# One core, fused Sinkhorn attention and ResMLP: reordering batch 0's loads, mixing and scoring, with other TensorE fillers

## The chip, the cores and the metric

The kernel runs on one core of one Trainium2 chip. The metric is the device time of one launch in microseconds (us). One core has five engines that run beside each other: TensorE (PE in the profile, with its weight loads shown apart as PEld), VectorE (DVE), ScalarE (ACT), GpSimd (POOL) and SyncE (SP). SP and POOL also issue the transfers (DMAs) from and to the chip's memory.

## What is computed

Four batches, eight heads, 768 positions, head size 64. For each head an 8x8 matrix goes through five rounds of a Sinkhorn normalisation; the result P mixes the eight blocks of 96 keys and of 96 values, each block of queries then attends to its own mixed block, and the output goes through a ResMLP block that mixes tokens and then channels.

```python
for _ in range(5):
    P = exp(P - max(P)); P = P / sum(P, -1); P = P / sum(P, -2)
k_sorted = einsum('bhij,bhjcd->bhicd', P, k_b)      # v_sorted the same
attn = softmax(scale * q_b @ k_sb.T)                 # inside each block of 96
x = (attn @ v_sb)  as (batch, 768, 512)
a1 = alpha1 * x + beta1
u = x + lam * einsum('ts,bsd->btd', w_tok, a1)
out = u + lam * (relu((alpha2 * u + beta2) @ w_ch1) @ w_ch2)
```

## The kernel before

The whole program is unrolled by Python: one straight list of instructions for each engine, which runs in the order in which the code issues it (the `Engine` wrapper at the top keeps that order). An engine waits at an instruction until its operands and its target buffer are free, and everything behind it on that engine waits too. There is no planner for batch 0: the order of its work is written out by hand at the end of the setup, from `mix_keys(0, psb)` down to `scale_affine(betaB)`. From there on a table (`put`, `run`) hangs the work of the next batch on the matmul groups of the present one: `h_unit` (the first channel product, 16 groups for each half of a batch) and `ch_unit` or `ch_pair` (the second).

Matmul results land in PSUM. Two pools hand out its tiles: psA has two slots of two banks, psB four slots of one bank. A new tile waits until the tile that last had its slot has been read.

Batch 0 goes through these steps, whose names the prediction uses:

- **Loads.** POOL issues the DMAs of q, k, v (each in two parts), of the token weights `wt16` (four parts), of alphaB, betaB and lamB, of W1p and W2p (four parts each) and of batch 1. All go into one queue. At most eight are under way, since a DMA that takes up the counter of an earlier one waits until that has landed.
- **Sinkhorn.** Five rounds, each one exponential on ACT and six small DVE operations. The table `beside` puts other work behind each round: `q_first` (24 small matmuls turn one group of queries), `q_out` (ACT copies them out), `mask` (DVE builds small masks from the identity), `prep_ab2`, and fillers.
- **Mixing.** `mix_keys` and `mix_values` make the matrices bigK and bigV from P. `k_turn` (24 matmuls of 64x64 for each of four groups) turns and mixes keys, `k_copy` copies them out. `v_sort` reorders the loaded values into VD in slices of eight or more of the 64 columns, `v_mix` (16 matmuls for each of eight slices) mixes them and copies them out to Vs.
- **Scores.** `score(0, g, half)` is eight matmuls and one exponential on ACT. There are four groups (pairs of heads) with two halves each. `pv_first(g)` is 24 matmuls that weight the values of a group, then a reciprocal and a multiplication on DVE that give x.
- **Token mixing.** `permute` reorders `wt16` into wp, `wtok` turns it (three matmuls) and copies it to w_tokT; `row_sum` and `row_sums` make the sums of the rows of the token weights; `first_mm`, `first_turn` and `first_finish` make, for one quarter of the channels at a time, the token product (tok_ps), the scaled input z and their sum a2T, which the first `h_unit` needs. `first_mm(3)` and `first_turn(3)` come after the first three h matmuls.
- **Fillers.** `warm(n)` and `fill` are matmuls of a tile of zeros, 128x512 in fp16, whose result nobody reads. They keep TensorE busy.

Before the change POOL issues k ahead of v, then makes the mask ebh, and does two of the four `v_sort` slices between the weight loads. ACT does two slices, and sums the rows of half of the token weights with three accumulating copies. DVE does the last slice and all the permuting. The eight `v_mix` stand between the scores of groups 0 to 2.

Of the kernel before, what the change touches and what calls it, by code (L numbers as in the profile page):

```python
# [16 lines left out]
def kernel(  # L17
# [111 lines left out]
    ebh = const([BH, B, 2, H, NB], F16, "ebh")  # L129

    def heads():
        for th in range(2):
            pool.tensor_copy(
                ebh[:, :, th, :, :],
                ident16[0:BH, 0:BH].rearrange("p (b h) -> p b h", h=H).unsqueeze(3).to_broadcast([BH, B, H, NB]),
            )
# [9 lines left out]
    )  # L146
    dve.memset(brow[:].bitcast(FT), 0.0)
    dve.memset(rrow[:].bitcast(FT), 0.0)
    load_slabs(k8, k)
    load_halves(v8, v[0])  # L150
    heads()
# [25 lines left out]
    pool.dma_start(alphaB[:], moe_alpha1.partition_broadcast(128))  # L177
    pool.dma_start(betaB[:], moe_beta1.partition_broadcast(128))
    pool.dma_start(lamB[:], moe_lam.partition_broadcast(128))
    v_sort(16, 32, pool.tensor_copy)  # L180
    for g in range(4):
        if g == 1:
            v_sort(48, 64, pool.tensor_copy)
        pool.dma_start(W1p[:, :, g * 512:(g + 1) * 512], w1v[:, :, g * 512:(g + 1) * 512])
    pool.tensor_tensor(brow[0:1, :], bet1[:], lam1[:], ALU.mult)

# [24 lines left out]
    def mask(n):  # L211
        if n == 0:
            dve.tensor_copy(ident16f[:], ident16[0:4 * CT, 0:4 * CT])
            dve.tensor_reduce(mlo[:], ident16[:].rearrange("p (b j) -> p j b", j=NB), AXX, ALU.add)
        elif n == 1:
            dve.tensor_reduce(msk[:], ident16[:].rearrange("p (b j) -> p b j", j=NB), AXX, ALU.add)
            dve.tensor_tensor(mhi[:], msk[:, 0:8], msk[:, 8:16], ALU.add)
            dve.tensor_reduce(mth[:], ident16[:].rearrange("p (th c) -> p th c", th=2), AXX, ALU.add)
        elif n == 2:
            dve.tensor_reduce(  # L220
                mgap[:], ident16[:].rearrange("p (th t) -> p th t", th=2)[:, :, 0:HB],
                mybir.AxisListType.XY, ALU.add,
            )

    def fill(out, n):
        for _ in range(n):
            pe.matmul(out, wz[:, 0:128], wz[:], start=True, stop=True)

# [45 lines left out]
    rcol = const([128, 3], FT, "rcol")  # L274

    def row_sum(m):
        if m == 0:
            a1_of[0] = moep.tile([128, 8, C], F16, name="a1", tag="a1", bufs=1)
        act.activation(a1_of[0][:].rearrange("p k c -> p (k c)")[:, 0:S], wt16[0][:, m, :], AF.Copy, accum_out=rcol[:, m:m + 1])


# [8 lines left out]
    def q_out(g):  # L290
        for half in range(2):
            q_copy(0, g, qps[g], half, act.copy)

    beside = {
        0: [lambda: q_first(0), lambda: warm(3)],
        1: [lambda: q_first(1), lambda: warm(2), lambda: warm(3)],
        2: [lambda: q_first(2), lambda: warm(3)],
        3: [lambda: q_out(0), lambda: q_first(3)],
        4: [lambda: q_out(1), lambda: q_out(2), lambda: q_out(3), lambda: prep_ab2(psb), lambda: warm(4)],
    }  # L300
    warm(12)
    for it in range(5):
        act.activation(P32[:], P32[:], AF.Exp)
        dve.tensor_reduce(rsum[:], P32[:], AXX, ALU.add)
        dve.reciprocal(rsum[:], rsum[:])
        dve.tensor_tensor(
            P32[:], P32[:], rsum[:].unsqueeze(2).to_broadcast([BH, NB, NB]), ALU.mult
        )
        dve.tensor_reduce(csum[:], P32[:].rearrange("p i j -> p j i"), AXX, ALU.add)
        dve.reciprocal(csum[:], csum[:])  # L310
        dve.tensor_tensor(
            (P16 if it == 4 else P32)[:], P32[:],
            csum[:].unsqueeze(1).to_broadcast([BH, NB, NB]), ALU.mult,
        )
        if it < 3:
            with nc.allow_low_precision(reason="sums of zeros and a one"):
                mask(it)
        for f in beside[it]:
            f()

    for g in range(4):
        pool.dma_start(W2p[:, g * 4:(g + 1) * 4, :], w2v[:, g * 4:(g + 1) * 4, :])

# [3 lines left out]
    def mix_keys(b, ps):  # L327
        rep = ps([128, H4, NB * NB], FT, "repk_ps")
        big = att.tile([128, H4, 64], F16, name="bigK", tag="bigK", bufs=2)
        for g0 in range(0, H4, 2):  # L330
            gs = slice(g0, g0 + 2)
            for g in range(g0, g0 + 2):
                for h2 in range(2):
                    n = b * H + 2 * g + h2
                    pe.matmul(
                        rep[h2 * 64:h2 * 64 + 64, g, :], ident16[0:BH, n:n + 1].to_broadcast([BH, 64]),
                        P16[:].rearrange("p i j -> p (i j)"), start=True, stop=True,
                    )
            sel = att.tile([128, 2 * NB, NB], FT, name="selk", tag="selk", bufs=2)
            dve.tensor_tensor(  # L340
                sel[:], rep[:, gs, :].rearrange("p g (i j) -> p (g i) j", j=NB),
                mhi[:].unsqueeze(1).to_broadcast([128, 2 * NB, NB]), ALU.mult,
            )
            red = att.tile([128, 2 * NB], FT, name="redk", tag="redk", bufs=2)
            dve.tensor_reduce(red[:], sel[:], AXX, ALU.add)
            dve.tensor_tensor(
                big[:, gs, :].rearrange("p g (i c) -> p (g i) c", c=NB),
                red[:].unsqueeze(2).to_broadcast([128, 2 * NB, NB]),
                mlo[:].unsqueeze(1).to_broadcast([128, 2 * NB, NB]), ALU.mult,
            )  # L350
        bigK[b] = big

    def mix_values(b, ps):
        rep = ps([128, NB * NB], FT, "repv_ps")
        pe.matmul(
            rep[:], ebh[:, b, :, :, :].rearrange("p a h j -> p (a h j)"),
# [4 lines left out]
            sel[:], rep[:].rearrange("p (i j) -> p i j", j=NB),  # L361
            mlo[:].unsqueeze(1).to_broadcast([128, NB, NB]), ALU.mult,
        )
        red = att.tile([128, NB], FT, name="red", tag="red", bufs=2)
        dve.tensor_reduce(red[:], sel[:], AXX, ALU.add)
# [3 lines left out]
            red[:].unsqueeze(1).to_broadcast([128, H, NB]), ALU.mult,  # L369
# [33 lines left out]
    def v_mix(b, n, ps, eng):  # L403
        ps = ps([128, 8, 64], FT, "v_ps")
        fill(ps[:].rearrange("p d x -> p (d x)"), 1 - n % 2)
        for s in range(8):
            for th in range(2):
# [3 lines left out]
                    ps[r, d, :], VD[r, n * 8 + d, :],  # L411
                    bigV[b][r, :, :].rearrange("p h i -> p (h i)"), start=True, stop=True,
                )
        eng(Vs[:, :, n * 8:(n + 1) * 8], ps[:].rearrange("p d x -> p x d"))
# [4 lines left out]
    def score(b, g, hf, ps):  # L419
        ps = ps([128, 2, 512], FT, "sc_ps")  # L420
        n = 128 if b == 0 else BLK
        keys = kT_of[b][:].rearrange("p g i t -> p (g i t)")
        for ii in range(4):
# [3 lines left out]
            for h2 in range(2):  # L427
                r = slice(h2 * 64, h2 * 64 + 64)
                pe.matmul(
                    ps[0:w, h2, ii * BLK:(ii + 1) * BLK], keys[r, lo:lo + w],  # L430
# [4 lines left out]
        act.activation(  # L435
            et[0:n].rearrange("p a i t -> p a (i t)"), ps[0:n, :, 0:4 * BLK], AF.Exp, scale=scale
        )
# [175 lines left out]
    def row_sums(ps):  # L613
        rc16 = const([128, 3], F16, "rc16")
        act.copy(rc16[:], rcol[:])
        ps = ps([1, 384], F16, "rr_ps")
        for m in range(3):
            pe.transpose(ps[:, m * 128:(m + 1) * 128], rc16[:, m:m + 1], ident16[:])
# [273 lines left out]

    mix_keys(0, psb)
    warm(3)
    mix_values(0, psb)
    prep_scales()
    dve.tensor_copy(Vs[:, :, D:GRP], mgap[:].unsqueeze(2).to_broadcast([128, H * NB, GRP - D]))
    kp0 = k_turn(0, 0, psb)
    kp1 = k_turn(0, 1, psb)
    k_copy(0, 0, kp0, 0, copy)  # L900
    k_copy(0, 0, kp0, 1, act.copy)
    warm(3)
    kp2 = k_turn(0, 2, psb)
    k_copy(0, 1, kp1, 0, copy)
    k_copy(0, 1, kp1, 1, act.copy)
    kp3 = k_turn(0, 3, psb)
    k_copy(0, 2, kp2, 0, copy)
    k_copy(0, 2, kp2, 1, act.copy)
    v_sort(0, 8, act.copy)
    v_sort(8, 16, act.copy)  # L910
    score(0, 0, 0, psa)
    k_copy(0, 3, kp3, 0, copy)
    k_copy(0, 3, kp3, 1, copy)
    score(0, 0, 1, psa)
    v_sort(32, 48, copy)
    warm(2, psb)
    v_mix(0, 0, psb, copy)
    v_mix(0, 1, psb, copy)
    score(0, 1, 0, psa)
    v_mix(0, 2, psb, copy)  # L920
    v_mix(0, 3, psb, act.copy)
    score(0, 1, 1, psa)
    v_mix(0, 4, psb, copy)
    v_mix(0, 5, psb, copy)
    score(0, 2, 0, psa)
    v_mix(0, 6, psb, copy)
    v_mix(0, 7, psb, act.copy)
    score(0, 2, 1, psa)
    row_sum(0)
    permute(0, copy, 0, 3)  # L930
    moe_start(0)
    warm(1, psb)
    pv_first(0)
    score(0, 3, 0, psa)
    wtok(0, copy)
    wtok(1, act.copy)
    wtok(2, copy)
    permute(0, copy, 3, 6)
    row_sum(1)
    row_sum(2)  # L940
    pv_first(1)
    wtok(3, copy)
    wtok(4, copy)
    wtok(5, copy)
    permute(1, copy, 0, 6)
    score(0, 3, 1, psa)
    pv_first(2)
    row_sums(psb)
    first_mm(0, psb)
    first_turn(0, psb)  # L950
    first_mm(1, psb)
    pv_first(3)
    first_turn(1, psb)
# [32 lines left out]
    for b in range(1, B):  # L986
        p = b - 1
        if b == 1:
            for n in range(3):
                put(0, 0, "h", 11 + n, lambda n=n: mix_v(1, n, act.copy))  # L990
                put(0, 0, "c", 3 + 3 * n, lambda n=n: mix_k(1, n, (act.copy,) * 4))
            put(0, 0, "h", 13, lambda: bounce_v(1))
# [112 lines left out]
```

## Time and profile before

| what | value |
|---|---|
| time, median of 3 runs | 258.61 us (258.02 to 258.95) |
| time of the profiled execution | 258.66 us |
| its span, first to last instruction | 256.9 us |
| outside the span | 1.8 us |
| PE busy | 246.9 us, 96% |
| DVE busy | 175.9 us, 68% |
| ACT busy | 155.3 us, 60% |
| POOL busy | 47.5 us, 18% |
| granted TensorE clock, mean | 0.997 |
| data moved by DMA | 31.07 MB, 121 GB/s over the span |

All times in the text are us from the start of the span, unless they are called durations. A line of the timeline gives the start, the duration, the engine, the operation with its tiles (result on the left of the arrow), the shape, the count of instructions merged into the line, and in brackets how long the engine stood idle before it and what it waited for. "issue" means that nothing the profile shows held the engine.

### The profile page before, as it was taken

To read this page: it belongs to the slowest core of one execution; us is meant where nothing else is said; L and a number is where in the kernel's file an instruction comes from. 1 tells how busy PE (TensorE), PEld (TensorE's weight loads), DVE (VectorE), ACT (ScalarE), POOL (GpSimd) and SP (SyncE) were. 2 spreads that over 40 slices of the span, in tenths; PEclk is the share of its full clock that TensorE was granted. 3 is DMA by queue.
4 is the path that set the end of the run, shared out by engine and by line. 5 is a ranking of instruction groups with operands and counts; after the bars stand their busy time and mean duration, and the time that the engine had idled before them with its cause. 6 is when DMAs were issued, how large, how long until landed. Compare 5 with 4: busy or idle time off the path is not lost.

```text
span 256.9 us, 5960 instructions
## 1 busy us (share of the span) xinstructions
PE 246.9 (96%) x2371; PEld 160.0 (62%) x2371; DVE 175.9 (68%) x467; ACT 155.3 (60%) x282; POOL 47.5 (18%) x73
## 2 busy tenths in 40 slices
PE   8998799999999999999999999999999999999994
PEld 2565565555555545456865787557756875686783
DVE  6696888594538956759896775298886873361873
ACT  3557767484997688496655587877465004847400
POOL 8859302810092010091000010000000000000000
PEclk9999999999999999999999999999999999999998
DMA  5999999997989997999972259910202232111023
GB/s 99 211 204 194 207 207 212 212 146 170 178 175 183 122 192 139 177 165 148 159 133 62 41 151 136 149 40 3 84 0 41 64 97 70 23 39 43 3 82 82
DMA packets 67535, 31.07 MB, mean 121 GB/s; under 512 B 56674, under 2 KB 63218, under 8 KB 67508
## 3 DMA queue, kind: packets, MB, share of 16 engines
q0 software_dynamic: 26832, 17.70, 46.9%
q1 hardware_dynamic: 40580, 12.97, 30.9%
q8 instruction: 18, 0.29, 0.5%
q14 instruction: 9, 0.07, 0.1%
q10 hardware_dynamic: 96, 0.03, 0.1%
HBM read 32.79 MB, written 8.65 MB: 161 GB/s over the span
## 4 chain that ended last, share of the span: by engine, by line
PE 81%; DVE 11%; ACT 4%; issue 2%; DVEq 0%
PE h_ps L65 28%; PE tok_ps L65 11%; PE px L65 8%; PE ch_ps L65 7%; PE pz L65 6%; PE py L65 5%; PE warm_ps L65 4%; PE x_ps L65 3%; DVE x L65 3%; PE sc_ps L65 2%; DVE ost L65 2%; DVE sums L65 2%; PE mix_ps L65 2%; PE kmix_ps L65 1%; PE v_ps L65 1%
## 5 line engine op out<-in xcount | busy, mean ns | idle before, releaser
L65 PE MATMUL h_ps<-a2T,W1p 128*128 128x384 bf16 x512 | 93.3, 326 | 0.0
L65 PEld LDWEIGHTS <-W1p 128*128 128x128 bf16 x512 | 47.9, 98 | 31.4 <-issue 0.4
L65 ACT ACTIVATE hTa<-h_ps 128x384 f16<-128x384 f32 x64 | 31.2, 493 | 30.3 <-PE h_ps L65 29.2
L65 ACT ACTIVATE hTb<-h_ps 128x384 f16<-128x384 f32 x64 | 31.2, 490 | 7.5 <-PE h_ps L65 7.5
L65 DVE SCALAR_TENSOR_TENSOR u<-tok_ps,x 128x512 f32<-128x512 f32 x21 | 14.5, 691 | 25.6 <-PE tok_ps L65 25.6
L65 PE MATMUL tok_ps<-a,w_tokT 128*128 128x512 f16 x126 | 30.3, 379 | 0.0
L65 ACT CAST kT<-kmix_ps 64x512 f16<-64x512 f32 x36 | 25.7, 713 | 5.7 <-PE kmix_ps L65 5.4
L65 ACT ACTIVATE et<-sc_ps 96x768 f16<-96x768 f32 (+1 forms) x32 | 24.8, 807 | 3.7 <-PE sc_ps L65 3.7
L65 ACT CAST u<-u 128x512 f16<-128x512 f32 x21 | 13.0, 618 | 21.3 <-DVE u L65 21.3
L65 PEld LDWEIGHTS <-sums 128*128 128x128 f16 x216 | 21.1, 98 | 3.5 <-issue 0.5
L65 PEld LDWEIGHTS <-hTa 128*128 128x128 f16 x192 | 18.4, 98 | 6.7
L65 PEld LDWEIGHTS <-hTb 128*128 128x128 f16 x200 | 18.6, 98 | 6.1
L65 PEld LDWEIGHTS <-w_tokT 128*128 128x128 f16 x126 | 12.3, 98 | 13.1 <-issue 0.2
L65 DVE TENSOR_TENSOR x<-x_ps,rcb 96x512 f16<-96x512 f32 x24 | 16.5, 686 | 0.8
L65 POOL DMA_DIRECT2D qn<-in_q_dram x18 | 16.0, 909 | 4.4 <-DMA raw<-in_v_dram 4.3
L65 DVE TENSOR_TENSOR sums<-hTa,hTb 128x512 f16<-128x512 f16 (+2 forms) x27 | 8.9, 330 | 10.3 <-ACT hTb L65 10.0
L65 PEld LDWEIGHTS <-et 96*128 96x128 f16 (+4 forms) x288 | 12.0, 100 | 4.7 <-DVE x L65 1.2
L65 PE MATMUL x_ps<-Vs,et 96*128 96x65 f16 (+4 forms) x288 | 13.0, 195 | 1.6 <-DVE x L65 0.9
L65 DVE SCALAR_TENSOR_TENSOR ost<-px,u 128x256 f32<-128x256 f32 x27 | 11.3, 419 | 3.4 <-PE px L65 3.4
L65 PE MATMUL warm_ps<-wz 128*128 128x512 f16 x36 | 11.8, 464 | 1.2 <-DVE wz L65 1.2
L65 POOL DMA_DIRECT2D vscr<-mixed x6 | 3.3, 557 | 48.0 <-ACT mixed L65 48.0
L65 PE MATMUL ch_ps<-W2p,hTb 128*128 128x512 f16 x48 | 11.8, 379 | 0.0
(140 smaller groups left out, 361.4 us busy)
## 6 DMA issues: line engine op xcount, KB each, us to landing
out_dram<-ost SPq DMA_DIRECT2D x23, 192.0 KB, 2.2
raw<-in_v_dram POOLq DMA_DIRECT2D x6, 384.0 KB, 7.4
raw<-in_k_dram POOLq DMA_DIRECT2D x6, 384.0 KB, 9.2
qn<-in_q_dram POOLq DMA_DIRECT2D x18, 128.0 KB, 10.6
vscr<-mixed POOLq DMA_DIRECT2D x6, 384.0 KB, 5.1
Vs<-vscr SPq DMA_DIRECT2D x3, 768.0 KB
W1p<-in_moe_w_ch_dram POOLq DMA_DIRECT2D x4, 512.0 KB, 11.2
W2p<-in_moe_w_ch_dram POOLq DMA_DIRECT2D x4, 512.0 KB, 17.1
```

The source lines that it names most:

```text
L65: ins = getattr(self.eng, name)(*args, **kwargs)
```

## The change

Only batch 0 and the setup are touched, and one detail of the mixing that all batches share.

- **Loads.** v is issued ahead of k. ACT makes the masks, a new one for the keys (ebk) among them, in place of POOL, between the first and the second exponential of the Sinkhorn rounds. alphaB, betaB, lamB, W1p and W2p are issued later on POOL, behind three `v_sort` slices and the product brow.
- **Fillers.** `slow(n)` is new: n matmuls of the same zeros read as fp32, 128x512. `slow(2)` and one `warm` take the place of the first twelve `warm`; single `slow(1)` stand beside rounds 1 to 3; `slow(2)` stands behind the scores of group 0. Of the other fillers one `warm` is left.
- **Mixing.** `mix_values` comes first. `mix_keys` works on all four groups at once (four matmuls and three DVE operations on 256 columns, where there were eight and six on 128). Their sums are kept in PSUM.
- **Values.** ACT sorts four slices of eight columns, POOL one of sixteen and two of eight. The matmuls of all eight slices (`v_mm`) and their copies (`v_out`, two slices in one copy once) come ahead of the scores, between the turns of the keys.
- **Scores.** Group 0 is scored between and behind the turns of the last keys, the other groups later. Four of the eight halves use two psB slots and two exponentials of 384 columns in place of one psA slot and one of 768.
- **Token weights.** All permuting goes from DVE to POOL, half 0 between the second and third part of W1p, half 1 behind the fourth part. The accumulating copies on ACT are gone; six matmuls with a column of ones sum the rows on TensorE.
- **Batch 1.** `mix_v` and `bounce_v` of batch 1 stand one h group later.

```diff
     def heads():
+        act.copy(ebk[:], ident16[0:BH, 0:H].unsqueeze(2).to_broadcast([BH, H, 64]))
         for th in range(2):
-            pool.tensor_copy(
+            act.copy(
...
+    load_halves(v8, v[0])
     load_slabs(k8, k)
-    load_halves(v8, v[0])
-    heads()
...
+    def slow(n, ps=psa):
+        z = wz[:].bitcast(FT)
+        out = ps([128, 512], FT, "warm_ps")
+        for _ in range(n):
+            pe.matmul(out[:], z[:, 0:128], z.unsqueeze(1).to_broadcast([128, 2, 256]), start=True, stop=True)
...
     beside = {
-        0: [lambda: q_first(0), lambda: warm(3)],
-        1: [lambda: q_first(1), lambda: warm(2), lambda: warm(3)],
-        2: [lambda: q_first(2), lambda: warm(3)],
-        3: [lambda: q_out(0), lambda: q_first(3)],
-        4: [lambda: q_out(1), lambda: q_out(2), lambda: q_out(3), lambda: prep_ab2(psb), lambda: warm(4)],
+        0: [heads, lambda: q_first(0), lambda: q_first(1)],
+        1: [lambda: slow(1), lambda: q_first(2)],
+        2: [lambda: q_out(0), lambda: slow(1)],
+        3: [lambda: q_out(1), lambda: q_out(2, 0), lambda: q_first(3), lambda: slow(1)],
+        4: [lambda: q_out(2, 1), lambda: q_out(3), lambda: prep_ab2(psb), lambda: gaps()],
     }
-    warm(12)
+    slow(2)
+    warm(1)
...
     def row_sums(ps):
-        rc16 = const([128, 3], F16, "rc16")
-        act.copy(rc16[:], rcol[:])
-        ps = ps([1, 384], F16, "rr_ps")
-        for m in range(3):
-            pe.transpose(ps[:, m * 128:(m + 1) * 128], rc16[:, m:m + 1], ident16[:])
+        ps = ps([1, 384], FT, "rr_ps")
+        for ks in range(NT):
+            pe.matmul(ps[:], ones[:], w_tokT[:, ks, 0:384], start=(ks == 0), stop=(ks == NT - 1))
         act.copy(rrow[0:1, :], ps[:])
...
+    mix_values(0, psb)
+    warm(1)
     mix_keys(0, psb)
-    warm(3)
-    mix_values(0, psb)
...
+    v_sort(48, 64, pool.tensor_copy)
+    v_sort(40, 48, pool.tensor_copy)
+    v_sort(32, 40, pool.tensor_copy)
+    for n in range(4):
+        v_sort(8 * n, 8 * n + 8, act.copy)
...
+    v0 = bank("v_ps")
+    v_mm(0, 0, v0)
+    v67 = psa([128, 1024], FT, "v_ps")[:]
+    v_mm(0, 6, v67[:, 0:512])
+    v_mm(0, 7, v67[:, 512:1024])
+    v12 = psa([128, 1024], FT, "v_ps")[:]
+    v_mm(0, 1, v12[:, 0:512])
+    v5 = bank("v_ps")
+    v_mm(0, 5, v5)
+    v_mm(0, 2, v12[:, 512:1024])
+    v_out(0, 1, v0, copy)
     kp0 = k_turn(0, 0, psb)
+    v_out(6, 2, v67, copy)
+    v4 = bank("v_ps")
+    v_mm(0, 4, v4)
+    v3 = bank("v_ps")
+    v_mm(0, 3, v3)
+    v_out(5, 1, v5, act.copy)
     k_copy(0, 0, kp0, 0, copy)
     k_copy(0, 0, kp0, 1, act.copy)
+    kp1 = k_turn(0, 1, psb)
...
+    score(0, 0, 0, psa)
+    kp2 = k_turn(0, 2, psb)
     kp3 = k_turn(0, 3, psb)
     k_copy(0, 2, kp2, 0, copy)
     k_copy(0, 2, kp2, 1, act.copy)
+    score(0, 0, 1, psa)
     k_copy(0, 3, kp3, 0, copy)
+    k_copy(0, 3, kp3, 1, act.copy)
+    slow(2)
+    prep_scales()
+    pool.tensor_tensor(brow[0:1, :], bet1[:], lam1[:], ALU.mult)
...
+    permute(0, pool.tensor_copy, 0, 6)
...
+    permute(1, pool.tensor_copy, 0, 6)
...
     score(0, 1, 0, psa)
+    score(0, 1, 1, psb)
+    pv_first(0)
     score(0, 2, 0, psa)
+    score(0, 2, 1, psb)
     wtok(0, copy)
+    wtok(1, copy)
+    pv_first(1)
+    score(0, 3, 0, psb)
+    pv_first(2)
     wtok(2, copy)
+    score(0, 3, 1, psb)
     wtok(3, copy)
+    wtok(4, act.copy)
     wtok(5, copy)
+    first_mm(0, psb)
     row_sums(psb)
+    pv_first(3)
+    first_mm(1, psb)
     first_turn(0, psb)
+    first_turn(1, psa)
     first_mm(2, psb)
```

## The prediction

> **What bounds the kernel now.** The page first: TensorE is busy nearly all the time and at full clock.
>
> ```profile
> PE 246.9 (96%) x2371; PEld 160.0 (62%) x2371; DVE 175.9 (68%) x467; ACT 155.3 (60%) x282; POOL 47.5 (18%) x73
> ...
> PEclk9999999999999999999999999999999999999998
> ...
> q8 instruction: 18, 0.29, 0.5%
> ```
>
> The last line is the instruction queue: 18 packets of 16 KB. Then the chain of work that ended last. From 40 us on it is matmuls almost without a break (PE 20.56 of the 20.90 us from 36.1 to 57), so what the change moves is worth what it does to the start of that stretch. The chain there reads:
>
> ```profile
> 36.13 0.58 ACT tok L65
> 36.72 0.57 ACT z L65
> 37.31 0.62 DVE a2T L65
> 37.93 0.60 DVE betaB L65
> 38.57 0.63 DVE a2T L65
> ```
>
> The last a2T ends at 39.19; behind it the first h group closes and the dense part begins. **39.19 is my yardstick**: a microsecond there is one at the end.
>
> Before it I looked for what holds TensorE, in the timeline:
>
> ```profile
> 20.98 0.40 PE L65 MATMUL v_ps<-bigV,vd 64*64 64x64 f16 x13
> ...
> 22.53 0.47 PE L65 MATMUL v_ps<-bigV,vd 64*64 64x64 f16 x19 [1.14 <-issue]
> ...
> 28.73 0.34 PE L65 MATMUL x_ps<-Vs,et 128*32 128x65 f16 x6 [0.66 <-issue]
> ```
>
> Two stops in the middle of a group, with nothing awaited. The table by stage, cut at them, counts the records (matmuls and weight loads; columns: busy us and count of each engine, clock, DMA share, GB/s):
>
> ```profile
> 0.00:22.00 22.00, 19.49 (x349) 10.22 (x350) 15.89 (x60) 11.91 (x25) 16.47 (x29) 1.00 0.98 172
> 22.00:28.50 6.50, 5.01 (x128) 3.85 (x128) 4.95 (x11) 5.01 (x10) 4.95 (x6) 1.00 1.18 207
> ```
>
> [...] With 6 semaphore records the first stop is at record 705, the next at 961. The transfers on q8 start at 13.1, 20.3, 26.3 and 32.8. Record 449 runs at 16.4 and record 705 can run at 22.5, 6.1 us later; 705 at 22.53, 961 at 28.72: 6.2 us. I take it that crossing one boundary asks for the code behind the next, and that it is there **6.2 us later** while the data queue is full (207 GB/s). Later blocks last over 9 us and never wait.
>
> [...]
>
> Last, what feeds the values:
>
> ```profile
> 15.37 0.54 POOL L65 DMA_DIRECT2D lamB<-in_moe_lam_dram  x1 [2.89 <-DMA v<-in_v_dram]
> 16.51 1.53 POOL L65 COPY vd<-v 128x768 f16<-128x768 f16 x1 [0.60 <-DMA v<-in_v_dram]
> 16.79 1.61 ACT L65 COPY vd<-v 128x384 f16<-128x384 f16 x2
> ```
>
> **Up to record 449.** *Sinkhorn.* ACT makes the masks behind the first exponential. ident is ready at 3.46; copies of 512, 256 and 256 columns, by Vs (0.59 for 512) and w_tokT (0.49 for 384), end at about 4.85, so the second exponential starts there, not at 4.09. The mask work on DVE is spread better and gives 0.2 back: P ends at 12.0, not 11.43. Its cover: the values. If they were there, 0.55 would be lost.
>
> *Values.* q lands at 7.9 as now. The v pair took 4.8 us behind k (11.6 to 16.5), so it lands at 12.8 (16.5 before); k then at 14.2 and 16.1. bigV is ready at 13.0 (three operations, 14.18 to 14.92, 0.74) and bigK at 14.3 (0.43 us a step). ACT's four slices at 0.81 each run 13.1 to 16.3, POOL's at 1.53, 0.77 and 0.77 to 16.1.
>
> *TensorE* follows in its order: slice 0 at 13.9, slices 6 and 7 at 14.6, 1 and 5 to 15.9, 2 to 16.3, then k_turn (0.5). The built program puts record 449 in the middle of that first turn: **16.6**, as good as before (16.4). The fillers saved are some sixty records, but their places are filled by values that can't come earlier.
>
> **The wait for code.** 16.6 + 6.2 = 22.8. One thing more: the request for block 449 itself falls, as now, at about 10.2 to 10.6, but then v's 6 KB packets are in the queue where k's 1.5 KB stood; the pair of v takes 4.8 us against 3.75 for k's. That delays 449 by 0 to 0.8; I take 0.3: record 705 runs at **23.1**. TensorE gets there at about 20.1: three more small groups, two turns, two halves of scores, paced by the DVE and ACT copies (0.64 and 0.51 each). It waits 3 us.
>
> **The two fp32 fillers.** The built list has one instruction for each fp32 matmul; the fp32 transposition (ab_ps) left a weight load and a matmul in the trace. Counted as two records, record 705 is just behind the scores of group 0, and slow(2) comes *after* the wait: it covers nothing and is paid in full. No row shows an fp32 product. Below: one pass as in fp16, 0.22 each when warm (three warm in 0.75), 0.43 for both. Above: both operands in two halves, four passes, 1.75 with a little between. I take the upper end, since the operands are twice as wide on both sides. [...] TensorE goes on at 24.85.
>
> **From there to the yardstick.** By the rows: six halves of scores at 0.3, four x at 0.93, six wtok at 0.17, three tok at 0.97, three turns at 0.35, and the row sums, new on TensorE: six matmuls of 384 columns at 0.16, 0.97 (three tiny transposes before). 11.5 us of TensorE in all, so 36.4 without waits. The waits:
>
> - x of group 1 wants the PSUM slot of group 0, whose DVE part (0.25 + 0.97) ends at 27.6: 0.35.
> - wtok 0 wants POOL's permuting. POOL is free of the values at 16.1, then brow (1.26), three broadcasts, two parts of W1p: 20.8. 2304 columns at 1.5 ns (ebh) to 2.0 ns (vd): done 24.3 to 25.4; wanted at 27.0. Hidden by 1.6 us, and a loss from 27.0 on.
> - wtok 3 to 5 and the DVE copies (0.3 each, behind x of groups 1 and 2) hold the token product to 32.0, about 0.5.
> - Record 961 comes at 30.2, its code at 23.1 + 6.2 = 29.3: no wait.
>
> The third turn ends at 37.25. ACT's z and tok (0.66 and 0.5) and DVE's a2T (0.62), alphaB and betaB (0.68) follow behind: the last a2T ends at 40.15. That is **0.95 later** than 39.19. DVE is rid of 2.9 us of permuting (0.88, 0.61, 1.40) and ACT of 3.1 us of row sums, but neither ended a wait here.
>
> **What costs nothing.** The data queue keeps its order and stays full, as W1p is issued at 20 for a queue that reaches it at 26; the weights land as before (28 to 46), and the later POOL issues (up to 34.5 for W2p) beat 35.9, when the queue would run dry. The four split exponentials cost ACT 0.42 + 0.49 for 0.81 each, which is in the times above; the mixing sums in PSUM lie, for batches 1 to 3, beside TensorE's h groups. mix_v one group later: Vs of batch 1 is back at 70.4, used at 73.8; up to 2 us later is hidden.
>
> **Sum.** 258.66 of the profiled execution (median 258.61) + 0.95 = **259.6**. A difference of 0.3%, 0.78 us, is about what a measurement of this kernel can tell from none.
>
> **Rivals.**
>
> 1. *The fillers hide in the wait*, because an fp32 matmul is one record or one pass. 1.3 to 1.7 come off; then record 961 waits for its code at 29.3 and gives some back: about **258.5**. For it: the build has them as one instruction. Against it: the two records of ab_ps.
> 2. *The wait for code goes*, because fewer fillers let the request out earlier. TensorE goes on at 20.1 + 1.75; now wtok 0 waits for POOL. At 1.5 ns it is there at 24.3: 2.35 off, **257.3**, faster than before; at 2.0 ns only 1.2 off. For it: 6.2 us is read from two stops in a full queue, and later packets on q8 came sooner. Against it: the queue is as full.
> 3. *The clock is cut* by the idle 3 us. Cold matmuls of 512 took 0.43 (twelve in 5.25), warm 0.22. If the clock falls at 23 for 3.4 us, half of that is lost: **261.3**. It decides once the stop is long enough; 1.34 us of idleness cut nothing here. [...]
>
> **Chances.** Forecast 0.38 (its own range 258.9 to 260.4), fillers hidden 0.17, no wait for code 0.23, clock 0.22. Faster by over 0.3%: 0.23. Within: 0.15 of the second case and 0.12 of the forecast, 0.27. Slower: 0.28 and 0.22, 0.50. The range takes in both ends: 257.3 with v landing a little sooner, 256.9; 261.3 with POOL at a slower rate or block 449 at its later end, 262.1.
>
> **What would show it.** A stop of about 3 us on TensorE at record 705, at 20 to 23, slow(2) right behind it, 1.7 us long; v landed at 12.8; wtok 0 not waiting; the last a2T at 40.1; clock at full from 10 us on. Wrong: a stop elsewhere or none, fp32 records of another length, a second slow stretch of the clock, or wtok behind POOL.

## The result and the profile after

The changed kernel takes **260.37 us** (median of 7 executions, 259.91 to 261.28), beside 258.95 (258.02 to 259.64) for the kernel before: ratio 1.0067, 95% interval 1.0041 to 1.0092. The profiled execution took 260.16, its span is 258.4. The forecast was 259.6, which is 0.95 us above the profiled execution of the kernel before. The kernel did become slower; the two profiled executions differ by 1.50.

The page of the changed kernel first. TensorE is as busy as before and the code comes in the same 18 packets, but the clock row has a 7 in its fourth slice.

```profile
PE 246.5 (95%) x2346; PEld 159.7 (62%) x2346; DVE 171.4 (66%) x454; ACT 156.7 (61%) x287; POOL 51.0 (20%) x76
...
PEclk9997999999999999999999999999999999999999
...
q8 instruction: 18, 0.29, 0.5%
```

The timeline of TensorE around the stop:

```profile
18.45 0.26 PE L65 MATMUL sc_ps<-qT,kT 64*128 64x96 f16 x3
20.73 0.28 PE L65 MATMUL sc_ps<-qT,kT 64*128 64x96 f16 x5 [2.03 <-issue]
20.95 2.83 PE L65 MATMUL warm_ps<-wz 128*128 128x512 f32 x4
23.71 0.82 PE L65 MATMUL sc_ps<-qT,kT 64*128 64x96 f16 x16
```

Record 705 stands inside the second half of the scores of group 0, after three of its eight matmuls. TensorE gets to that record at 18.50 and goes on at 20.73, with nothing awaited; 2.03 us of that are idle by the trace. Then the two fp32 fillers run from 20.95 to 23.70, 2.75 us. They are four matmuls in the trace, not two. The clock explains their length; the table by stage, cut as for the kernel before, has the mean clock in the column behind the five engines:

```profile
0.00:22.00 22.00, 16.49 (x357) 9.71 (x358) 15.13 (x56) 14.53 (x32) 18.28 (x29) 1.00 0.97 171
22.00:28.50 6.50, 6.21 (x106) 4.04 (x105) 2.13 (x6) 3.57 (x8) 6.50 (x9) 0.74 1.19 206
```

0.74 is half speed for 3.41 us, from 21.95 to 25.36 in the trace's clock records. The chain at the yardstick:

```profile
36.36 0.60 DVE a2T L65
36.96 0.50 issue
37.45 0.68 DVE alphaB L65
38.14 0.53 DVE a2T L65
38.67 0.60 DVE betaB L65
39.27 0.02 DVEq L65
39.28 0.04 issue
39.33 0.63 DVE a2T L65
```

The last a2T ends at **39.95**, 0.76 later than 39.19. The h matmuls behind it stand 0.76 later than in the kernel before, up to 100 us (0.33 later for those around 55 us, where the mixing of batch 1's values has moved). Then the distance grows to 1.28 at 104 us and to 1.50 at 125 us, and stays. So the loss has two halves, and the second one was not in the prediction. At 103 us the timeline of DVE shows a wait that the kernel before does not have; here is its line, then that of the changed kernel:

```profile
101.99 1.25 DVE L65 TENSOR_SCALAR a2T<-uT,ab2col 128x384 bf16<-128x384 f16 x4
```

```profile
103.27 1.25 DVE L65 TENSOR_SCALAR a2T<-uT,ab2col 128x384 bf16<-128x384 f16 x4 [0.59 <-DMA uT<-u]
```

SP issues the transfer that makes uT. Its timeline in the kernel before, then in the changed one:

```profile
83.98 9.78 SPq L65 DMA_TRANSPOSE qT<-qn  x6
93.85 2.83 SPq L65 DMA_DIRECT2D out_dram<-ost  x2
96.77 3.81 SPq L65 DMA_TRANSPOSE uT<-u  x3
```

```profile
85.22 10.83 SPq L65 DMA_TRANSPOSE qT<-qn  x6
96.14 1.83 SPq L65 DMA_DIRECT2D out_dram<-ost  x2
98.06 3.81 SPq L65 DMA_TRANSPOSE uT<-u  x3
```

The transpositions of batch 2's q start 1.24 us later (0.76 of it the shift) and end 2.3 later: two of the six took 2.3 and 3.3 us and the others 1.2; in the kernel before those two took 2.3 and 2.2. The two issues of output stores behind them took 1.0 less, so the u transpositions, next in SP's order, start 1.29 later, and a2T 1.28 later. The first q transposition waits for batch 2's q, whose loads POOL issues behind a copy from Vs, the tile that batch 1's values come back to (the "gate"). POOL's store of the values and its gate, in the kernel before and in the changed one:

```profile
56.96 1.11 POOL L65 DMA_DIRECT2D vscr<-mixed  x2 [5.87 <-ACT mixed L65]
70.64 0.18 POOL L65 COPY gate<-Vs 1x1 f16<-1x1 f16 x1 [12.57 <-DMA Vs<-vscr]
```

```profile
58.59 1.10 POOL L65 DMA_DIRECT2D vscr<-mixed  x2 [7.20 <-ACT mixed L65]
72.44 0.18 POOL L65 COPY gate<-Vs 1x1 f16<-1x1 f16 x1 [12.74 <-DMA Vs<-vscr]
```

The store is 1.63 later and the gate 1.80, of which 0.76 is the shift. The rest I put down to the move of the store by one h group; the experiments below try that. The last 0.22, at 115.7 us, is one of three copies on DVE (1.45 us for the three, 1.23 before); why it is slower stays open.

### The profile page after: what moved, and what is told of

It is laid out like the page before. It is cut to its first block, busy times and chain, and to the rows that moved or that the text cites. A ratio compares the mean times of both kernels' runs of the same rounds, so it can differ in the third digit from the quotient of the medians.

```text
span 258.4 us, 5908 instructions
## 1 busy us (share of the span) xinstructions
PE 246.5 (95%) x2346; PEld 159.7 (62%) x2346; DVE 171.4 (66%) x454; ACT 156.7 (61%) x287; POOL 51.0 (20%) x76
## 4 chain that ended last, share of the span: by engine, by line
PE 74%; DVE 15%; ACT 4%; issue 3%; SPq 2%; DMA 1%; POOL 1%; DVEq 0%; POOLq 0%
PE h_ps L65 27%; PE tok_ps L65 10%; PE px L65 8%; PE pz L65 5%; PE ch_ps L65 5%; PE py L65 5%; PE x_ps L65 3%; PE sc_ps L65 2%; DVE x L65 2%; DVE sums L65 2%; SPq L65 2%; PE mix_ps L65 2%; DVE ost L65 1%; PE kmix_ps L65 1%; DVE a2T L65 1%
## 5 line engine op out<-in xcount | busy, mean ns | idle before, releaser
L65 ACT ACTIVATE et<-sc_ps 96x768 f16<-96x768 f32 (+2 forms) x36 | 25.1, 738 | 7.5 <-PE sc_ps L65 7.5
L65 PEld LDWEIGHTS <-kT 64*128 64x128 f16 (+1 forms) x256 | 6.7, 97 | 10.9 <-issue 8.4
L65 PE MATMUL sc_ps<-qT,kT 64*128 64x96 f16 (+1 forms) x256 | 10.3, 209 | 3.3 <-issue 2.0
```

Of the source, the lines that this page charges most:

```text
L65: ins = getattr(self.eng, name)(*args, **kwargs)
```

## The experiments

**Theory A**: the first half is the stop for code, the fillers that run behind it, and the cut clock. **Rival B**: the fillers fill time that TensorE would wait anyway. **Theory D**: the second half is the later store of batch 1's values, by way of SP. **Rival E**: it is the shift alone.

In all the experiments the 33 transposing transfers (q of batches 2 and 3, and u) are plain copies of the same bytes, so these tiles stand unturned and the values that follow from them are not the reference's. The first comes at 54 us, so the stage up to the yardstick is untouched. The second half had to be tried with stand-ins; with the transposing transfers themselves the move was not tried by itself.

The column "cut" counts the executions whose mean clock is 0.993 or less: one stretch of 3.41 us at half clock takes 0.0066 off the mean of 257 us. The ratio is to the kernel before, executed beside each group of runs: before_plain to filler_ahead are one group, late_turn, one_rowsum, hold_wtok and mixv_back_plain a second, dve_rowsum, after_two and mixv_two a third, before_two a fourth. Across groups the ratios are compared, not the medians.

| run | median us (range) | cut | last a2T | ratio (95%) |
|---|---|---|---|---|
| changed kernel | 260.37 (259.91 to 261.28) | 7 of 7 | 39.95 | 1.0067 (1.0041, 1.0092) |
| before_plain | 258.42 (257.69 to 260.04) | 5 of 12 | 39.59 | 0.9983 (0.9963, 1.0003) |
| after_plain | 259.87 (258.45 to 260.86) | 10 of 12 | 40.75 | 1.0034 (1.0014, 1.0053) |
| no_tail | 258.73 (257.93 to 259.18) | 12 of 12 | 38.17 | 0.9990 (0.9972, 1.0008) |
| filler_ahead | 258.56 (258.30 to 258.93) | 5 of 12 | 38.23 | 0.9981 (0.9960, 1.0002) |
| late_turn | 258.21 (257.75 to 259.05) | 0 of 12 | 38.50 | 0.9986 (0.9969, 1.0003) |
| one_rowsum | 258.96 (258.07 to 259.85) | 8 of 12 | 38.96 | 1.0006 (0.9985, 1.0026) |
| dve_rowsum | 257.68 (256.73 to 260.42) | 4 of 12 | 38.65 | 0.9966 (0.9941, 0.9990) |
| hold_wtok | 260.74 (260.15 to 263.68) | 5 of 6 | 38.75 | 1.0101 (1.0059, 1.0142) |
| mixv_back_plain | 260.33 (257.90 to 261.79) | 10 of 12 | 41.18 | 1.0057 (1.0030, 1.0083) |
| after_two | 261.50 (258.60 to 262.52) | 7 of 8 | 41.48 | 1.0089 (1.0054, 1.0123) |
| mixv_two | 260.77 (259.39 to 262.48) | 6 of 6 | 41.78 | 1.0082 (1.0049, 1.0115) |
| before_two | 258.53 (258.01 to 259.06) | 2 of 12 | 38.97 | 0.9976 (0.9956, 0.9996) |

The a2T column is one profiled execution each. Record 449 runs between 14.9 and 16.8 in them, so the column is best read against the place of the stop in the same run.

### The base: before_plain and after_plain

```diff
-        sp.dma_start_transpose(
-            qT_of[b][:, :, kt * 128:(kt + 1) * 128], qn_of[b][:, kt, :, :].rearrange("p h d -> p (h d)"),
+        sp.dma_start(
+            qT_of[b][:, :, kt * 128:(kt + 1) * 128], qn_of[b][:, kt, :, :].rearrange("p (g a) d -> p g (a d)", a=2),
         )
```

(and the same for uT). Expected of before_plain:

> The kernel before with its 33 transposing transfers (q of batches 2 and 3, and u) made into plain copies of the same bytes, so that these tiles stand unturned in this and in all the runs below. The first of them comes at 54 us, so the last a2T should stay at 39.2 and the stops at records 705 and 961 as they are. Later SP should be done sooner and waits on uT at 102 us go: a base some us from 258.9 on either side, for the comparison with the next run.

Expected of after_plain:

> The changed kernel with the same plain copies. Last a2T at 39.95 as in the changed kernel, 0.76 later than the kernel before. Theory D (the half microsecond that the change loses at 103 us is SP's transpositions coming late): against the run before_plain only the 0.76 us stay, ratio to it 1.003. Rival E (it is lost elsewhere behind 40 us): 1.4 to 1.5 us stay, ratio 1.0055.

The medians differ by 1.45 us, as Rival E has it. The traces say otherwise: the two profiled executions differ by 1.16 at the last a2T and by 1.16 to 1.20 at the h matmuls from there to the end, so in these two **next to nothing is lost behind 40 us** once SP's transfers are short. The medians mix executions with a cut clock and without, 10 of 12 with one in after_plain and 5 of 12 in before_plain. Among those with a cut the medians are 259.97 and 258.95, 1.02 apart; among those without 258.84 (two alone, 258.45 and 259.23) and 258.22, 0.62 apart. Both are nearer to the traces than to the 1.4 to 1.5 of Rival E.

### The fillers: no_tail and filler_ahead

```diff
     k_copy(0, 3, kp3, 1, act.copy)
-    slow(2)
     prep_scales()
```

> The run after_plain without the two fp32 fillers behind the scores of group 0. Theory A (the stop for code, the cut clock behind it, and the fillers that run after the stop make the loss): the fillers' 2.75 us (20.95 to 23.70) go; the code still comes at 20.7, the clock is still cut at about 22 for 3.4 us, now over work in place of fillers, which costs about 1 us more than in the changed kernel; last a2T 1.5 to 2.2 us sooner than 39.95 (37.8 to 38.5), and the median as much below after_plain. Rival B (the fillers only fill time in which TensorE would wait for the exponentials, the copies or POOL's permuting): last a2T and median less than 0.7 us sooner.

The timeline of no_tail, at the stop and at 61 us:

```profile
18.40 0.26 PE L65 MATMUL sc_ps<-qT,kT 64*128 64x96 f16 x3
20.70 0.62 PE L65 MATMUL sc_ps<-qT,kT 64*128 64x96 f16 x21 [2.05 <-issue]
21.89 1.00 PE L65 MATMUL x_ps<-Vs,et 128*128 128x65 f16 x24 [0.56 <-ACT et L65]
...
60.91 0.23 PE L65 MATMUL qt_ps<-ident,qn 128*128 128x128 f16 x1 [0.24 <-DMA qn<-in_q_dram]
62.04 0.23 PE L65 MATMUL qt_ps<-ident,qn 128*128 128x128 f16 x1 [0.90 <-DMA qn<-in_q_dram]
```

The scores of group 1 follow the stop at once; the last a2T is at 38.17, inside the 37.8 to 38.5 of Theory A and 1.8 before the changed kernel's. Rival B falls. But the median gains only 1.14 against after_plain: a new wait at 61 us, for batch 1's last q, gives part of it back (the distance to after_plain shrinks from 2.58 at the yardstick to 1.1).

The other run keeps the fillers, ahead of the stop:

```diff
+    slow(2)
     score(0, 0, 1, psa)
     k_copy(0, 3, kp3, 0, copy)
     k_copy(0, 3, kp3, 1, act.copy)
-    slow(2)
```

> The run after_plain with the same two fp32 fillers ahead of the second half of the scores of group 0, so that they run before record 705 instead of behind it. Theory A: they fill 1.7 us of the 2.2 us stop, which shrinks to about 0.7 us, the clock stays at full, the code still comes at 20.7; last a2T about 3 us sooner than 39.95 (36.8 to 37.5), about 1 us better than with the fillers left out, and that difference is the price of the cut clock. Rival B: at most 0.7 us sooner. Rival C (the code comes a fixed time after TensorE gets to the end of its block, not after the crossing before it): the stop stays 2.2 us long behind the fillers, and nothing is gained over leaving them out.

The timeline of TensorE in filler_ahead:

```profile
18.39 1.55 PE L65 MATMUL warm_ps<-wz 128*128 128x512 f32 x3
21.05 0.59 PE L65 MATMUL warm_ps<-wz 128*128 128x512 f32 x1 [1.11 <-issue]
21.57 0.68 PE L65 MATMUL sc_ps<-qT,kT 64*128 64x96 f16 x24
22.82 1.00 PE L65 MATMUL x_ps<-Vs,et 128*128 128x65 f16 x24 [0.56 <-ACT et L65]
```

Six of the fillers' eight records run before record 705, which now lies in them; the code comes at 21.05 (20.70 without the fillers) and the stop is 1.11 us long, not 2.2, so Rival C falls. The clock stays at full in this profile and in 7 of 12 executions (in no_tail in none). The last a2T is at 38.23, not at 36.8 to 37.5 as expected: one matmul of filler still runs behind the stop (0.52), and x waits 0.56 for the exponential, as it does in no_tail. From the first score behind the stop to the last a2T it takes 16.66 us here and 17.47 in no_tail, 0.81 more with the clock cut: that is the **price of the cut** over work, as near as two runs tell it. The medians, 258.56 and 258.73, do not show it, since both then wait for q at 61 us.

### Where the gain went: late_turn

On top of filler_ahead, the first two turns of batch 1's q stand later:

```diff
-                put(0, 0, "c", (4, 7, 10, 10)[g], lambda g=g: q_turn_late(1, g, (dve.tensor_copy, act.copy)[g % 2]))
+                put(0, 0, "c", (7, 8, 10, 10)[g], lambda g=g: q_turn_late(1, g, (dve.tensor_copy, act.copy)[g % 2]))
```

> The run filler_ahead with the first two turns of batch 1's q (the transpositions by TensorE into qt_ps) three steps and one step later in the first ch unit (steps 7, 8, 10, 10 for 4, 7, 10, 10). In filler_ahead 2.5 us are gained at the last a2T and 1.3 of them are given back at 62 us, where the first of these turns waits for the last q transfer of batch 1 to land (61.99). Theory G (that wait is all that takes the gain back): the wait goes, the offset of -2.5 us against after_plain stays to the end, median 257.3 to 257.5, 1.1 below filler_ahead. Rival H (another transfer of the full data queue is next: raw k, the values' way through the store, or the loads of batch 2): median above 258.2.

The wait on q is gone from the profile, and of the distance to after_plain, 2.25 at the last a2T, 1.98 is left at the end. That is Theory G in the trace, nearly. In the times it is not: 1.1 below filler_ahead was expected, and the ratios are 0.9986 and 0.9981, no gain at all, with no clock cut in any execution and a spread of 1.3 us. What varies between these executions stays open; no trace shows a wait that would be Rival H.

### The row sums: one_rowsum and dve_rowsum

In one_rowsum, on top of after_plain, the sums over five of the six key tiles are left out:

```diff
-        for ks in range(NT):
-            pe.matmul(ps[:], ones[:], w_tokT[:, ks, 0:384], start=(ks == 0), stop=(ks == NT - 1))
+        pe.matmul(ps[:], ones[:], w_tokT[:, 0, 0:384], start=True, stop=True)
```

> The run after_plain with one of the six matmuls of the row sums; the sums over the other five key tiles are left out. Theory A with TensorE as the bound from 31 to 40 us: five matmuls of 0.17 go, the last a2T comes 0.8 us sooner, median 0.8 below after_plain (259.1). Rival F (ACT and DVE pace the tok, turn and a2T steps): last a2T moves by less than 0.3 us, median above 259.5.

From the end of the fillers to the last a2T it takes 14.84 us (24.12 to 38.96), in after_plain 15.66 (25.09 to 40.75): 0.82 less, the five matmuls; in both the clock is at full over that stretch. By the ratios, 1.0006 and 1.0034, the whole is some 0.7 us faster. Rival F falls; TensorE bounds this stretch.

So the sums were put where there is room, on top of late_turn:

```diff
     prep_scales()
+    dve.tensor_reduce(rcol[:], wt16[0][:], AXX, ALU.add)
+    copy(rc16[:], rcol[:])
...
-        for ks in range(NT):
-            pe.matmul(ps[:], ones[:], w_tokT[:, ks, 0:384], start=(ks == 0), stop=(ks == NT - 1))
+        for m in range(3):
+            pe.transpose(ps[:, m * 128:(m + 1) * 128], rc16[:, m:m + 1], ident16[:])
```

> The run late_turn with the row sums taken by one reduction on DVE (2304 columns, in its idle time from 19.4 to 23.9 us) and three tiny transpositions on TensorE in place of six matmuls of 384 columns. Theory A with TensorE as the bound from 31 to 40 us: some 0.9 us less on TensorE, last a2T 0.8 to 0.9 us sooner than in late_turn, median 257.3 to 257.5, below both kernels. Rival H (the data queue is what bounds the stretch behind 40 us by now: q, raw or the values' way through the store land too late): last a2T sooner as above, but a new wait between 58 and 75 us and a median above 257.9.

DVE, in its idle time before the first x:

```profile
22.16 2.55 DVE L65 TENSOR_REDUCE rcol<-wt 128x3 f32<-128x2304 f16 x1
24.75 0.36 DVE L65 CAST rc<-rcol 128x3 f16<-128x3 f32 x1
25.09 0.23 DVE L65 RECIPROCAL rc<-x_ps 128x12 f32<-128x12 f32 x1
```

From the first score behind the fillers to the last a2T: 15.84 us (22.81 to 38.65), 0.81 less than in late_turn (21.85 to 38.50). The last a2T itself is no sooner than in late_turn, as record 449 ran 1.4 us later in this execution (16.67 and 15.30). This is the fastest version, 257.68, a little above the 257.3 to 257.5 expected, ratio to the kernel before 0.9966 (0.9941 to 0.9990). It has the plain copies, so the fair neighbour is before_plain with its 0.9983 (0.9963 to 1.0003). By these ratios it is some 0.4 us faster than that, and the intervals overlap.

### Why the code is late: hold_wtok

On top of after_plain, the four loads of w_tok are issued behind POOL's copies of v.

```diff
-        for lo, n in ((0, 96), (TAIL, 32)):
-            pool.dma_start(
...
+    def load_wtok(half):
+        for lo, n in ((0, 96), (TAIL, 32)):
+            pool.dma_start(
...
     v_sort(32, 40, pool.tensor_copy)
+    for half in range(2):
+        load_wtok(half)
```

> The run after_plain with the four loads of w_tok issued behind POOL's copies of v (at 15.3 to 17.8 us instead of 6 to 9.8), so that the data queue runs empty when k has landed at 16.6. Theory A (the code waits behind the data in the queue: asked for at the crossing of record 449 at 15.3 to 16.1, it comes when what is ahead of it is through): the code packet is through at about 17.7 instead of 19.4 to 20.0, record 705 runs without a stop or with one below 0.7 us, TensorE goes on from the fillers 1.5 to 3 us sooner; of that POOL's permuting, now late, takes about 1 us back at wtok 0; last a2T 0.5 to 2 us sooner. Rival I (the code takes some 5.5 us whatever is in the queue): stop and record 705 as in after_plain, last a2T later by the permuting.

The table by stage, for the microsecond from 16 to 17, first of after_plain, then of hold_wtok; the last column is what the data engines moved, in GB/s:

```profile
16.00:17.00 1.00, 1.00 (x46) 1.00 (x44) 0.31 (x2) 0.53 (x2) 1.00 (x2) 0.50 1.16 210
```

```profile
16.00:17.00 1.00, 1.00 (x46) 0.83 (x39) 1.00 (x3) 1.00 (x4) 1.00 (x2) 1.00 0.47 45
```

With the queue run dry, TensorE goes on like this:

```profile
18.36 0.34 PE L65 MATMUL sc_ps<-qT,kT 64*128 64x96 f16 x8
18.64 1.98 PE L65 MATMUL warm_ps<-wz 128*128 128x512 f32 x4
20.55 0.51 PE L65 MATMUL sc_ps<-qT,kT 64*128 64x96 f16 x16
...
24.37 0.51 PE L65 MATMUL wtok_ps<-ident,wp 128*128 128x128 f16 x6 [1.90 <-POOL wp L65]
```

Record 449 runs at 15.17, the code packet asked for there is through at 16.83 (19.42 in the changed kernel), and record 705 runs at 18.42 **with no stop at all**. The packet itself takes as long as in the changed kernel (0.94 and 0.97 us) but starts 0.72 us after record 449 and not 3.20. Theory A holds and Rival I falls: the code waits behind the data that is queued ahead of it. The last a2T is at 38.75 although wtok waits 1.9 us for POOL. The time is 260.74 all the same: batch 1's q is loaded later, and four of its turns wait for it at 61 to 64 us, which turns a lead of 1.8 us on after_plain into a lag of 0.95.

### The second half: mixv_back_plain, after_two, mixv_two, before_two

```diff
-                put(0, 0, "h", 12 + n, lambda n=n: mix_v(1, n, act.copy))
+                put(0, 0, "h", 11 + n, lambda n=n: mix_v(1, n, act.copy))
...
-            put(0, 0, "h", 14, lambda: bounce_v(1))
+            put(0, 0, "h", 13, lambda: bounce_v(1))
```

> The run after_plain with the mixing of batch 1's values and their store back in the h groups where the kernel before has them (11 to 13 and 13). Theory D (the move puts the store, and behind it Vs of batch 1, the gate and the loads of batch 2, about 0.9 us later than the shift of the whole stretch): store issued at 58.5 instead of 59.4, Vs landed and the loads of batch 2 issued 0.8 to 0.9 us sooner; no change of the median here, where the transpositions on SP that the loads delay are plain copies. Rival E (the store is late by the shift alone): all of them as in after_plain. Either way a store that is in the data queue sooner may push the last q of batch 1, as in no_tail: then up to 1 us slower.

The same two lines of POOL, in after_plain and in mixv_back_plain:

```profile
59.39 1.10 POOL L65 DMA_DIRECT2D vscr<-mixed  x2 [7.45 <-ACT mixed L65]
73.60 0.18 POOL L65 COPY gate<-Vs 1x1 f16<-1x1 f16 x1 [13.11 <-DMA Vs<-vscr]
```

```profile
58.95 1.10 POOL L65 DMA_DIRECT2D vscr<-mixed  x2 [6.58 <-ACT mixed L65]
72.29 0.18 POOL L65 COPY gate<-Vs 1x1 f16<-1x1 f16 x1 [12.24 <-DMA Vs<-vscr]
```

This execution runs 0.43 behind after_plain, and the store is still 0.44 earlier: 0.87 against the stretch, as Theory D says; the gate gains 1.7. The end gains nothing, as expected with short transfers: the distance stays at 0.4.

So SP's time per transfer was put back, by cutting each plain copy in two halves (0.6 us each on SP; a transposition took 1.2), q's in the same way:

```diff
-            sp.dma_start(
-                uT[:, :, m * 128:(m + 1) * 128], u16_of[b][:, 3 * hf + m, :].rearrange("p (c x) -> p c x", c=CT),
-            )
+            for x in (slice(0, 2), slice(2, 4)):
+                sp.dma_start(
+                    uT[:, x, m * 128:(m + 1) * 128], u16_of[b][:, 3 * hf + m, :].rearrange("p (c x) -> p c x", c=CT)[:, x],
+                )
```

> The run after_plain with each plain copy that stands for a transposing transfer cut in two halves, so that SP spends about 1.2 us on each, as on a transposition (0.6 in after_plain). Theory D (the 0.5 us that the changed kernel loses at 103 us is SP's time: the q transpositions of batch 2, started late, hold the u transpositions behind them): u of batch 1 lands later than in after_plain, a2T at 103 us waits for it, 0.3 to 0.6 us are lost there: median about 260.3. Rival J (it was the transposing transfers' own time in the data engines, not SP's): as after_plain, 259.9.

> The run after_two with the mixing of batch 1's values and their store back in the h groups of the kernel before (11 to 13 and 13). Theory D: the loads of batch 2 and with them the first q transfer on SP are about 0.9 us sooner against the stretch, the wait on uT at 103 us is gone or 0.4 us shorter; median 0.3 to 0.5 below after_two. Rival E: same as after_two.

> The kernel before with each plain copy cut in two halves, as in after_two: the control for it. Theory D (the transfers on SP are late only in the changed kernel): no wait of DVE on uT at 102 us, offset against before_plain below 0.2 us at 104 us, median within 0.4 us of before_plain (258.4), and so 2.5 us or more below after_two. Rival K (SP's longer transfers hold this kernel as well): a wait of DVE on uT at 102 us and 0.5 us or more lost there, median above 259.0; the half microsecond then belongs to the transfers and not to the change.

DVE's a2T of batch 1, in after_two, in mixv_two and in before_two:

```profile
105.13 1.36 DVE L65 TENSOR_SCALAR a2T<-uT,ab2col 128x384 bf16<-128x384 f16 x4 [0.90 <-DMA uT<-u]
```

```profile
104.87 1.36 DVE L65 TENSOR_SCALAR a2T<-uT,ab2col 128x384 bf16<-128x384 f16 x4 [0.35 <-DMA uT<-u]
```

```profile
101.63 1.25 DVE L65 TENSOR_SCALAR a2T<-uT,ab2col 128x384 bf16<-128x384 f16 x4
```

The wait comes back in after_two, and 1.1 us with it between 100 and 106 us (the distance to after_plain goes from 0.71 to 1.82, and to 2.17 behind 126), more than the 0.3 to 0.6 expected. The kernel before has no such wait and does not feel the halves at all (ratios 0.9976 and 0.9983): Rivals J and K fall. With the store one group earlier the wait is 0.55 shorter, and the distance to after_two goes from +0.30 to -0.27 there; at the end it is -0.08. That is the move's share of the wait, 0.55 of 0.90, as one trace of each shows it. In time, 260.77 and 261.50 with spreads of 3 to 4 us do not tell the two apart.

## Why the prediction was right or wrong

**The yardstick** held: 0.76 at the last a2T was still 0.76 at the h matmuls 60 us later. The forecast there was 0.95.

**Up to record 449**: 15.25, not 16.6. v landed at 12.09 (12.8 forecast) and P was ready at 11.65 (12.0), so bigV and its copies were early too.

**The wait for code**: the place was right. That the stops are waits for code was my reading of the rows; hold_wtok shows it, where the packet is through at 16.83 and the stop is gone. It took 5.5 us from record 449 until TensorE went on at 705, not 6.2 + 0.3; in the kernel before it took 6.1 (16.43 to 22.53), in late_turn 6.0 (15.30 to 21.33). TensorE reached 705 at 18.50 (20.1 forecast) and went on at 20.73 (23.1). The stop was 2.2 us, not 3.

**The two fp32 fillers**: behind the stop and covering nothing, as forecast; 1.75 was the right price at full clock (0.43 for each of the four matmuls). Two of the four ran at half clock: 2.75. The count of records was wrong: each filler is two weight loads and two matmuls.

**From there to the yardstick**: 16.25 us (23.70 to 39.95) instead of 15.3, as the clock was at half up to 25.36. From 23.70 to there that is 1.66 us at half clock, which can cost 0.83 at most. wtok 0 did not wait; POOL's first half was done at 22.1, not 24.3 or later, at 1.0 ns for a column. Record 961 did not wait. The row sums took 1.06 (0.97 forecast) and were on the path in full (0.82 for five sixths).

**The third rival** happened in place of the forecast's clock "at full": the stop cut the clock. Its price was put at half of 3.4 us, 1.7. No row that stands with the forecast shows these 3.4 us; the changed kernel's clock records have 3.41 (21.95 to 25.36). The price was, in the changed kernel, 1.0 on the fillers and up to 0.83 on the work behind them, and in no_tail, where work stood in the fillers' place, some 0.8. The code, 2.4 us earlier than forecast, paid for it. Against the forecast, TensorE went on 2.37 sooner at the stop, took 1.22 more up to the end of the fillers (0.22 of it scores that the forecast had ahead of the stop) and 0.95 more from there to the last a2T: 0.20 less in all. So **the 0.95 came out near 0.76 by luck**, by errors of opposite sign: "clock at full from 10 us on" was wrong, and the stop was taken to end too late. **Rivals 1 and 2** fell: the fillers did not hide, and the wait did not go.

**The step that failed** is "mix_v one group later: ... up to 2 us later is hidden". I looked at one reader of Vs, TensorE at 73.8, and not at POOL's gate, which holds the loads of batch 2, the q transpositions on SP and the u transpositions behind those. That chain lost 0.52 us at 103 us, and DVE 0.22 behind it: 0.74 of the 1.50 in the profile, which the forecast has at nothing. With stand-ins for the transfers, the wait is SP's (after_two has it, after_plain and before_two do not), and the move of the store is 0.55 of its 0.90 (mixv_two still waits 0.35). What the rest is, the plain shift or another part of the change, is not shown. So Theory D holds for the larger part of the wait, and Rival E falls as the whole cause but not for the smaller part.

## What to carry to other kernels

Before a filler is put anywhere, count the records to the next stop for code. Here fillers ahead of the stop cost about half a microsecond and kept the clock up in 7 of 12 executions (in none of 12 without them); behind the stop they were paid in full, and two of their four matmuls at half clock. A store or load that is moved should be followed through every queue behind it, not only to the engine that reads the data. And what is won in an early stage is worth only what the transfers of the next one allow: here 1.1 of 2.5 us in the trace, until the reader of the late load was put behind other work.

## What the runs showed of the hardware

- **Clock.** The clock records of the kernel before show full clock from 6.27 to 255.44, 249.17 us; those of the changed kernel full clock from 4.89 to 21.95 (17.07 us), half clock to 25.36 (3.41) and full clock to 257.47 (232.11). These lengths are 73, 5, 1 and 68 times 3.41 us. I divided both runs into stretches of 3.41 us, counted from these changes, and took the share of each that the matmul rows cover. In the changed kernel the stretch ahead of the half clock, 18.54 to 21.95, has 40%; in it TensorE was idle for 2.03 us at record 705. At the end of the two runs half clock followed stretches with 22% (changed) and 38% (before). In the kernel before the two stretches with the stops have 66% (19.92 to 23.34; 1.34 us between the records at 705, 1.14 idle by the timeline) and 62% (26.74 to 30.15), and full clock went on. But before_plain stopped for 1.39 us, and its clock was cut: a filler of 128x512 took 0.61 us behind the stop (23.47) and 0.39 ahead of it (20.52). In filler_ahead the stop was 1.11 us and the profiled execution stayed at full clock. In hold_wtok, with no stop at 705 and a wait of 1.90 us for POOL, 5 of 6 executions had a cut. So at which share half clock follows, and whether the share is the measure at all, stays open.
- **Code.** The two stops of the kernel before are 256 records apart (128 matmuls and 128 weight loads from 22.00 to 28.50), and each of the 18 packets on its instruction queue has 16384 bytes. From record 449 until the packet of code asked for there was through it took 4.2 us behind a full data queue in the changed kernel (15.25 to 19.42), 4.8 in the kernel before (16.43 to 21.25) and 1.7 with the queue running dry (15.17 to 16.83 in hold_wtok, where the stop at record 705 is gone).
- **fp32.** A 128x512 product of fp32 tiles is four records in the changed kernel (two weight loads and two matmuls), 0.86 us at full clock (0.43 for one matmul, 21.48 to 21.91) and 1.70 before the clock is up (0.85 for one, 2.21 to 3.06). That is four times the fp16 one in the kernel before (0.22, 8.35 to 8.57, and 0.43, 2.02 to 2.45).
